# Sine tables in pairs: the second table of each pair taken from the first one's angle, and k's pad written by a transfer

## The chip, the cores and the metric

The kernel runs on one core of a Trainium2 chip. The metric is the device time of one execution in microseconds (us). Before the change the median of three runs is 212.61 us (212.39 to 212.65). Five engines work side by side, each in the order of its own program: TensorE (PE, with its weight loads PEld) multiplies matrices into PSUM, VectorE (DVE) and ScalarE (ACT) compute element by element and can read PSUM, GpSimd (POOL) makes masks and small constants and issues some transfers, SyncE (SP) issues most transfers.

## The reference

The function computes two independent branches on sequences of 2048 tokens with 576 channels and joins them along the channels.

```python
# branch A: attention in a sliding window of 8 positions, 2 apart, 32 heads of 18
qkv = x @ wqkv
idx = pos[:, None] - off[None, :]
logits = where(idx >= 0, einsum(q, k[idx]) * 18 ** -0.5, -1e9)
a = einsum(softmax(logits), v[idx]) @ wo

# branch B: a long convolution per channel
k_shift = sum(k_pad[:, t:t + S, :] * shift_k[:, 3 - t] for t in range(4))   # k_pad: three rows of zeros first
kv = k_shift * v
y = irfft(rfft(kv, 2S) * rfft(ssm_k, 2S))[:, :S] + kv * ssm_D
b = q * y
```

All inputs and the output are bf16. Three rows of zeros ahead of k are what the change calls k's pad.

## The kernel before, in words

Branch A is projections (`project_first`, lines 494 to 504, and `project`, 373 to 423), products of q and shifted k on VectorE with sums on TensorE (`logits`), a softmax, weighted sums of v (`weigh`) and the output projection (`output`). Branch B splits the sequence into four blocks of 512 tokens. For each block, `taps` (571 to 597) multiplies k's shifted rows by the tap table `skb` and then by v on VectorE; `mirror` folds the block on TensorE (L606); `x_spectrum` and `filter_spectrum` turn the blocks and the filter into the frequency domain with matmuls against tables of sines and cosines; `products` multiplies them, and `inverse` goes back with the tables `TI`, which `table_i` (449 to 460) makes from the x tables by matmuls (L455).

The order of the work is written out by hand. Each engine runs its instructions in the order in which the program emits them. From line 545 on, TensorE's units are put into a list `units` and taken from it by counts in constants such as `PLACES`; the change touches none of these. The prefix ahead of that, lines 519 to 544, is straight code: the tap table is spread by three calls of `spread_taps` (L513 matmuls, L516 evacuations by ScalarE), the x rows of the first two quarters are transposed (L467, L472; copied out by VectorE at L527 and by ScalarE at L528, L538 and L477), and four `project_first` run (L500 and L502 matmuls, an evacuation by ScalarE at L504 behind each). Sines are placed between these evacuations:

```python
    sines = [table_k(0), table_k(1)]            # 521: integer work on VectorE is emitted here
    ...
    sines += [table_x(0), table_x(1)]           # 531: and here
    ...
    project_first(0, 2)
    sines[2]()                                  # the sine itself, on ScalarE
    for n in range(2):
        project_first(1, 2 * n)
        sines[3 - 3 * n]()
```

The last table, `sines[1]`, follows the first evacuation of `project` (`with_sine`, 554 to 560). A call of `table` emits two multiply-adds (L438) and one bitwise and (L439) on VectorE, which give the phases of two vectors of 512 as integers, and returns the sine (L440) as a function: one activation of 128 x 1024, from int32 in `Ks` to bf16 in `TB`. Pools of PSUM: tag A and tag B, with two buffers each. Projections, `table_i` and the tap table's larger parts take buffers of tag A, transposes and folds those of tag B. A unit that takes a buffer waits until the buffer's former content has been evacuated.

Queues: SyncE issues x, wqkv, k and v for the front in the order of the calls in lines 196 and 244 to 259. `load_k` (198 to 215) brings k's rows for one block into `kj`, 7 rows per partition; block 0's first partition has the three rows of zeros ahead of it, which GpSimd writes with a memset (L205) before it issues the transfer of the four rows behind them (L206). The tile `xw` starts with 512 columns of zeros (L161), which serve the warming matmuls of `idle_work`; the first tap of block 0 (L577) later writes its result over them.

Of the kernel before, what the change touches and what calls it, by code (L numbers as in the profile page):

```python
# [11 lines left out]
ACT = mybir.ActivationFunctionType  # L12
ALU = mybir.AluOpType
FP32 = mybir.dt.float32
# [39 lines left out]
def view(t, offset, dims):  # L54

    return bass.AP(tensor=t.tensor, offset=t.offset + offset, ap=[list(t.ap[0])] + [list(d) for d in dims])
# [3 lines left out]
def kernel(  # L60
# [13 lines left out]
    nc = tc.nc  # L74
# [28 lines left out]
    HB = 4 * D  # L103
# [23 lines left out]
    xw = main.tile([128, 12 * HB], BF16, name="xw")  # L127
    XO = 8 * BL
    TB = main.tile([128, XO + 4 * BL], BF16, name="TB")
    TK = view(TB, 0, [[2 * BL, 2], [BL, 2], [1, BL]])  # L130
    TX = view(TB, XO, [[BL, 4], [1, BL]])
# [19 lines left out]
    def load_w(eng, comp, to=None):  # L151
        low, high = (to[:, 0:4, :], to[:, 4, :]) if to is not None else \
            (view(xw, w_at(0, comp), [[D, 4], [1, D]]), wq(4, comp, 0, D))
        eng.dma_start(low, A_wqkv[0:512, comp * D:(comp + 1) * D].rearrange("(kb p) a -> p kb a", p=128))
        for r in range(2):
            eng.dma_start(high[64 * r:64 * r + 64, :], A_wqkv[512:576, comp * D:(comp + 1) * D])

    s1 = ExitStack()
    sp1 = s1.enter_context(tc.tile_pool(name="s1", bufs=1, reuse_waits="tile"))
    zeros = view(xw, 0, [[1, 512]])  # L160
    nc.vector.memset(zeros, 0.0)  # L161
    pib = main.tile([128, 1], FP32, name="pib")
# [3 lines left out]
    nc.scalar.dma_start(skrow[96:97, :], B_shift_k.rearrange("d j -> (d j)").unsqueeze(0))  # L166
    warm = sp1.tile([128, 1], FP32, name="warm")
    nc.scalar.activation(warm[:], pib[:], ACT.Sin)
    ones96 = sp1.tile([97, 256], BF16, name="ones96")
    nc.vector.memset(ones96[:], 0.0)  # L170
    nc.vector.memset(ones96[96:97, 0:128:2], 1.0)
# [10 lines left out]
    Ks = main.tile([128, 12 * HB], BF16, name="Ks")  # L182
    xnat = view(Ks, 4 * HB, [[HB, 4], [D, 4], [1, D]])
    n_all = view(Ks, 8 * HB, [[1, 4 * HB]]).bitcast(I32).rearrange("p (n f) -> p n f", n=9)
# [8 lines left out]
    def load_x(qtr):  # L193
        nc.sync.dma_start(xnat[:, qtr], xf[512 * qtr:512 * qtr + 512, :].rearrange("(sb p) c -> p sb c", p=128))
# [3 lines left out]
    def load_k(i):  # L198

        eng = nc.sync  # L200
        kj = sp1.tile([128, 7, D], BF16, name="kj", bufs=2)
        r0 = BL * i
        low = [(0, 64)]
        if i == 0:
            nc.gpsimd.memset(kj[0:1, 0:3, :], 0.0)  # L205
            nc.gpsimd.dma_start(kj[0:1, 3:7, :], kf[0:4, :].unsqueeze(0))  # L206
            low = [(1, 49), (49, 64)]
        for a, b in ((3, 7), (0, 3)) if i == 0 else ((0, 7),):
            for p0, p1 in low:
                eng.dma_start(kj[2 * p0:2 * p1:2, a:b], bass.AP(  # L210
                    tensor=kf.tensor, offset=kf.offset + (r0 + 4 * p0 - 3 + a) * D,
                    ap=[[4 * D, p1 - p0], [D, b - a], [1, D]]))
            eng.dma_start(kj[1:128:2, a:b], bass.AP(tensor=kf.tensor, offset=kf.offset + (r0 + 256 + 3 - a) * D,
                                                    ap=[[4 * D, 64], [-D, b - a], [1, D]]))
        kjs.append(kj)
# [15 lines left out]
    rp = main.tile([128, 8], FP32, name="rp")  # L231
# [11 lines left out]

    load_w(nc.sync, 0)
    load_x(1)

    def turn_x(h):

        r0 = 1024 + 512 * h
        nc.sync.dma_start(xnat[:, 2 + h, :, 512:576], xf[r0:r0 + 512, 512:576].rearrange("(sb p) c -> p sb c", p=128))  # L250
        nc.sync.dma_start_transpose(view(xw, 6 * HB + 512 * h, [[1024, 4], [1, 512]]), xf[r0:r0 + 512, 0:512])

    load_k(0)
    load_w(nc.sync, 1)
    load_v(0)
    load_k(1)
    turn_x(0)
    turn_x(1)
# [16 lines left out]
    for h in range(2):  # L275
        f = fold[:, 64 * h:64 * h + 64]
# [156 lines left out]
    nc.vector.tensor_copy(rp[:], rp_i[:])  # L433
    nc.vector.tensor_scalar(rp[64:128, 4:8], rp[64:128, 4:8], -510.0, None, op0=ALU.add)

    def table(n_i, T, vec, cols, period, offs):
        for n in range(2):
            nc.vector.tensor_scalar(n_i[:, n, :], vec, rp[:, cols[n]:cols[n] + 1], offs[n], op0=ALU.mult, op1=ALU.add)  # L438
        nc.vector.tensor_single_scalar(n_i, n_i, period - 1, ALU.bitwise_and)  # L439
        return lambda: nc.scalar.activation(T, n_i, ACT.Sin, bias=pib[:], scale=-2.0 * np.pi / period)  # L440

    def table_k(c):
        return table(n_all[:, 2 * c:2 * c + 2, :], TK[:, c, :, :], n_all[:, 8, :], (2 + c, 2 + c), 2048, (256.0, 1792.0))

    def table_x(n):
        return table(n_all[:, 4 + 2 * n:6 + 2 * n, :], TX[:, 2 * n:2 * n + 2, :], n_all[:, 8, :], (4, 5), 4096,
              (512.0 + 1024.0 * n,) * 2)

    def table_i(s):

# [28 lines left out]
    def pair_x():  # L479
        return pp.tile([128, 2, 1024], BF16, name="ps_x", tag="B")  # L480
# [13 lines left out]
    def project_first(jp, ct0):  # L494

        ps = bank2("ps_proj", "A")
        for e in range(2):
            c0 = 128 * (ct0 + e)
            for kb in range(4):
                nc.tensor.matmul(ps[:, e, :], wq(kb, 0, c0, 128), xT(kb, 512 * jp, 512), start=(kb == 0), stop=False)  # L500
        for e in range(2):
            nc.tensor.matmul(ps[:, e, :], wq(4, 0, 128 * (ct0 + e), 128)[64 * jp:64 * jp + 64],  # L502
                             x5(0)[64 * jp:64 * jp + 64], start=False, stop=True, tile_position=(64 * jp, 0))
        nc.scalar.activation(view(q, S * ct0 + 512 * jp, [[S, 2], [1, 512]]), ps[:], ACT.Copy)  # L504

    def spread_taps(n0):
        n = min(256, D - n0)
        ps = bank2("ps_sk", "A" if n == 256 else "B")
        for h in range(0, n, 128):
            w = min(128, n - h)  # L510
            sk = skrow[:, 4 * (n0 + h):4 * (n0 + h + w)].rearrange("p (d j) -> p d j", j=4)
            for r in range(2):
                nc.tensor.matmul(ps[:, h // 128, 0:4 * w], ones96[:, 128 * r:128 * r + 128],  # L513
                                 sk if r else view(skrow, 4 * (n0 + h) + 3, [[4, w], [-1, 4]]),
                                 start=(r == 0), stop=(r == 1))
        nc.scalar.activation(skb[:, :, n0:n0 + n],  # L516
                             ps[:].rearrange("p b (d j) -> p j (b d)", j=4)[:, :, 0:n], ACT.Copy)

    spread_taps(512)
    spread_taps(0)  # L520
    sines = [table_k(0), table_k(1)]
    pts = [pair_x() for _ in range(2)]
    for n in range(2):
        transpose_x(0, pts[n], 2 * n, range(4))
# [3 lines left out]
        nc.scalar.activation(xT(2 + n, 0, 512), pts[1][:, n, 0:512], ACT.Copy)  # L528
    copy_tail(0, pts[1])
    spread_taps(256)  # L530
    sines += [table_x(0), table_x(1)]
    project_first(0, 0)
    pts = [pair_x() for _ in range(2)]
    for n in range(2):
# [125 lines left out]
    def fold_filter(m):  # L660
        kt, swapped = kTok(m), m < 2

        def unit():
            assert m in signed
            minus = minus_of(m)
            pss = [bank2("ps_rev", "A") for _ in range(2)]
            for c in range(2):
                turns = [((flip2r, flip1)[c] if swapped else flip0, 1 - c), ((identn0, identn)[c], 2 + c)]
                if not swapped:
                    turns.insert(1, ((corner2, corner)[c], c))  # L670
                for n, (w, of) in enumerate(turns):
                    for h in range(2):
                        nc.tensor.matmul(pss[c][:, h, 0:HD], w[:], kt[:, of, HD * h:HD * h + HD], start=(n == 0),  # L673
                                         stop=(n == len(turns) - 1))
            for c in range(2):
                nc.scalar.activation(halves(kt[:, c, :]), pss[c][:, :, 0:HD], ACT.Copy, scale=0.5)
                pe(0.5, "A", 0.65)
            nc.gpsimd.dma_start(view(Ks, k_at(m, 2) + 2 * D, [[1, 2 * D]]), view(Ks, k_at(m, 2), [[1, 2 * D]]),
                                accum_op=ALU.add, max_dma_last_dim=2 * D)
            nc.gpsimd.dma_start(other(m)[1:128], kt[1:128, 0, :], accum_op=ALU.add)  # L680
            nc.gpsimd.dma_start(other(m)[0:1], minus, accum_op=ALU.add)

        return (1.0, unit, f"fold{m}")
# [21 lines left out]
    def made(f, *args):  # L705
        n = len(units)
        f(*args)
        return [units.pop() for _ in range(len(units) - n)][::-1]
# [13 lines left out]
    for i in range(NBL):  # L722
# [4 lines left out]
        if i < 2:  # L727
            load_k(i + 2)
            load_v(i + 2)
# [14 lines left out]
        if i == 3:  # L744
            need("fold3")
            first = made(filter_spectrum, 3)
            now = deque(first)
            first = [[now.popleft() for _ in range(min(n, len(now)))] for n in EARLY]
            now, first = first[0] + [fold_filter(2)] + first[1] + mirrors[:1] + first[2] + mirrors[1:], list(now)
# [3 lines left out]
        for n, u in enumerate(mirrors):  # L753
            n = AT[n] if n < 2 else AT[i]
# [591 lines left out]
```

## Time and profile before

| | |
|---|---|
| median of three runs | 212.61 us |
| the profiled execution's own time | 212.5 us |
| its span, first to last instruction | 210.8 us |
| granted TensorE clock, mean | 0.998 |
| busy: TensorE, VectorE, ScalarE, GpSimd | 95%, 92%, 71%, 35% of the span |
| transfers | 39.66 MB, mean 188 GB/s |

The page of the profile and its views give times in microseconds from the span's start; L12 is line 12 of the kernel's file. In the timeline, a row has start, busy time, engine, line, operation, output and input, the number of instructions merged into it, and in brackets the idle time of the engine ahead of it with what ended it. In groups by line, the figures behind the bar are busy time and mean nanoseconds of one, then the idle time ahead of them. The chain of waits follows the work that ended last back from the end, at each step to what released it. A matmul's busy time is modelled and matmuls overlap, so a busy TensorE is not one at its peak.

### The profile page before, as it was taken

Reading aid. Unit: us, or ns where it says so; the run is one execution under the profiler, and the core shown is the slowest. Engines: PE = TensorE matmul, PEld = TensorE weight load, DVE = VectorE, ACT = ScalarE, POOL = GpSimd, SP = SyncE. Lnnn points to the kernel's source line nnn. Section 1 sums busy time; section 2 is a strip of 40 time slices with the busy share of each in tenths; the row PEclk is TensorE's granted clock in tenths of the full one; section 3 lists DMA queues with packets and bytes.
Section 4 is the critical chain, followed back from the end, with each engine's and each line's share of the span. In section 5 each row is a group of like instructions: output and inputs, shape, how many; then the busy total and the mean of one; then the engine's idle time right before and its main releaser. Section 6 shows DMA issues by size and latency. Waiting matters only on the chain.

```text
span 210.8 us, 5106 instructions
## 1 busy us (share of the span) xinstructions
PE 200.1 (95%) x2114; PEld 110.7 (53%) x2122; DVE 193.1 (92%) x146; ACT 150.5 (71%) x218; POOL 74.0 (35%) x111
## 2 busy tenths in 40 slices
PE   7999999999999999899999999999989999999891
PEld 2443443344554656564354666656555666666460
DVE  7989999999999999858889999999999849999981
ACT  3799988657684989986369788855666796775540
POOL 8999993001195516320175000002029004033000
PEclk9999999999999999999999999999999999999999
DMA  6999998999639336999999997587559995985133
GB/s 201 303 328 231 266 342 280 170 192 182 151 75 122 48 40 87 180 181 171 235 225 238 194 234 159 105 208 185 153 223 255 239 322 110 214 243 182 28 113 111
DMA packets 35396, 39.66 MB, mean 188 GB/s; under 512 B 17619, under 2 KB 29007, under 8 KB 35374
## 3 DMA queue, kind: packets, MB, share of 16 engines
q1 hardware_dynamic: 26812, 24.88, 47.2%
q0 software_dynamic: 6096, 11.96, 30.4%
q10 hardware_dynamic: 2466, 2.51, 3.5%
q8 instruction: 16, 0.26, 0.5%
q14 instruction: 6, 0.05, 0.1%
HBM read 13.11 MB, written 4.72 MB: 85 GB/s over the span
## 4 chain that ended last, share of the span: by engine, by line
PE 80%; ACT 10%; DVE 5%; issue 2%; DVEq 0%; ACTq 0%
PE ps_proj L378 16%; PE ps_z L1126 9%; PE ps_wo L1029 8%; PE ps_acc L973 7%; PE ps_inv L1158 7%; PE ps_fx L776 6%; PE ps_log L847 4%; PE ps_proj L500 3%; PE ps_fk L627 3%; PE ps_proj L382 3%; PE ps_proj L389 3%; ACT Ks L695 3%; PE ps_rev L673 2%; PE ps_fk L628 1%; ACT qk L977 1%
## 5 line engine op out<-in xcount | busy, mean ns | idle before, releaser
L378 PE MATMUL ps_proj<-xw 128*128 128x512 bf16 x153 | 37.4, 380 | 0.6 <-issue 0.3
L832 DVE TENSOR_TENSOR av<-qk 128x4096 bf16<-128x4096 bf16 (+1 forms) x16 | 31.7, 2013 | 2.8 <-PE ps_log L847 2.8
L378 PEld LDWEIGHTS <-xw 128*128 128x128 bf16 x160 | 14.0, 97 | 20.5 <-issue 6.2
L1099 DVE TENSOR_TENSOR qk<-xw,Ks 128x2304 bf16<-128x2304 bf16 x14 | 18.5, 1355 | 2.5 <-PE ps_inv L1158 2.4
L1139 ACT ACTIVATE av<-ps_z 128x768 bf16<-128x768 f32 x20 | 15.3, 808 | 6.2 <-PE ps_z L1126 6.2
L414 ACT ACTIVATE qk<-ps_proj 128x1024 bf16<-128x1024 f32 x14 | 14.3, 1023 | 7.6 <-PE ps_proj L389 3.3
L695 ACT ACTIVATE Ks<-ps_fk 128x576 bf16<-128x576 f32 x32 | 18.6, 717 | 1.3 <-PE ps_fk L628 1.3
L577 DVE TENSOR_TENSOR tB<-kj,skb 128x4608 bf16<-128x4608 bf16 (+1 forms) x8 | 19.3, 2417 | 0.1
L778 ACT ACTIVATE xw<-ps_fx 128x576 bf16<-128x576 f32 x32 | 18.4, 666 | 0.0
L776 PE MATMUL ps_fx<-xw,TB 128*128 128x288 bf16 x128 | 18.0, 286 | 0.2
L1055 POOL DMA_DIRECT2D Ks<-Ks x3 | 3.7, 1218 | 41.1 <-PE ps_wo L1029 28.7
L1029 PE MATMUL ps_wo<-qk 128*128 128x288 bf16 x128 | 17.8, 287 | 0.0
L627 PE MATMUL ps_fk<-Ks,TB 128*128 128x384 bf16 x62 | 16.9, 326 | 0.8 <-ACT Ks L695 0.7
L414 ACT ACTIVATE v<-ps_proj 128x1024 bf16<-128x1024 f32 x9 | 9.3, 1029 | 9.3 <-PE ps_proj L378 4.3
L973 PE MATMUL ps_acc<-av,ident 64*64 64x512 bf16 x160 | 15.3, 377 | 0.0
L628 PE MATMUL ps_fk<-Ks,TB 128*128 128x192 bf16 x62 | 15.2, 245 | 0.0
L776 PEld LDWEIGHTS <-TB 128*128 128x128 bf16 x128 | 12.0, 97 | 6.0 <-issue 2.9
L1029 PEld LDWEIGHTS <-qk 128*128 128x128 bf16 x128 | 11.6, 98 | 5.6 <-issue 3.0
L1158 PE MATMUL ps_inv<-av,TI 128*128 128x288 bf16 (+1 forms) x96 | 13.6, 293 | 0.6 <-ACT av L1139 0.6
L1161 ACT ACTIVATE v<-ps_inv 128x576 bf16<-128x576 f32 (+1 forms) x14 | 9.5, 677 | 6.3 <-PE ps_inv L1158 6.3
L977 ACT ACTIVATE qk<-ps_acc 128x1024 bf16<-128x1024 f32 x8 | 8.2, 1024 | 8.0 <-PE ps_acc L973 8.0
L956 DVE TENSOR_TENSOR av<-Ks,v 128x4096 bf16<-128x4096 bf16 x6 | 13.6, 2286 | 0.2 <-PE ps_acc L973 0.2
(199 smaller groups left out, 471.3 us busy)
## 6 DMA issues: line engine op xcount, KB each, us to landing
Ks<-Ks POOLq DMA_DIRECT2D x9, 576.0 KB, 7.1
TB<-av SPq DMA_DIRECT2D x12, 256.0 KB, 5.5
kj<-in_B_k_dram SPq DMA_DIRECT2D x6, 504.0 KB, 6.1
vt<-in_B_v_dram SPq DMA_DIRECT2D x8, 288.0 KB, 5.2
Ks<-av SPq DMA_DIRECT2D x8, 256.0 KB, 5.5
Ks<-Ks SPq DMA_DIRECT2D x3, 576.0 KB, 6.1
Ks<-in_A_x_dram SPq DMA_DIRECT2D x2, 576.0 KB, 5.2
xw<-in_A_wqkv_dram SPq DMA_DIRECT2D x2, 576.0 KB, 5.9
```

The costliest lines, as they stand in the source:

```text
L378: nc.tensor.matmul(ps[:, jp, :], wq(kb, comp, 128 * ct, 128), xT(kb, 1024 * jj + 512 * jp, 512), **se)
L414: nc.scalar.activation(view(t, o + pad + 1024 * jj, [[512, 2], [1, 512]]), ps[:], ACT.Copy)
L577: dve(2304 * n, lambda: nc.vector.tensor_tensor(to, view(kj, row * D, [[D, n], [D, 4], [1, D]]), view(skb, row * D, [[D, n], [0, 4], [1, D ...
L627: nc.tensor.matmul(o[:, 0:2], w, rhs[:, 0:2], start=start, stop=stop)
L695: nc.scalar.activation(view(Ks, k_at(m, cs ^ (m & 1)) + 96 * gi, [[768, 3], [384, 2], [1, 96]]), acc3(ps), ACT.Copy, scale=(PSG, MSG)[cs][ ...
L776: nc.tensor.matmul(ps[:, pm, 0:HD], TX[:, 2 * pm + c, 128 * gi:128 * gi + 128], kv[:, 2 * c + pm, HD * h:HD * h + HD], start=(c == 0), sto ...
L832: return P, at, step, dve(1024 * nj, lambda: nc.vector.tensor_tensor(view(P, at, [[step, 4], [256, nj], [1, 256]]), view(t, o + 256 * hh, ...
L973: nc.tensor.matmul(acc[64 * o:64 * o + 64, h, :], ident[64 * h:64 * h + 64, 64 * h:64 * h + 64], view(P, 256 * u, [[2048, 2], [1, 256]])[6 ...
L1029: nc.tensor.matmul(ps[:, r, 0:HD], oT(hh, 2 * c + r, t)[:, o:o + 128], wo[:, t // 2, t % 2, HD * h:HD * h + HD], start=(t == 0 and h == 0) ...
L1099: r = dve(3 * QTR, lambda: nc.vector.tensor_tensor(pr, view(xw, HB * XG[i] + QTR * t, [[HB, 3], [1, QTR]]), view(Ks, k_at(j - i, 0) + QTR ...
L1126: nc.tensor.matmul(view(acc[r], 512 * h, [[192, 2], [96, 2], [1, 96]])[o:o + 64], w[64 * h:64 * h + 64, 64 * h:64 * h + 64], pr[64 * h:64 ...
L1158: nc.tensor.matmul(ps[:, c, 0:n], TI[:, sl, pm, 128 * c:128 * c + 128], Y(j, pm)[:, sl, c0:c0 + n], start=(pm == 0 and sl == 0), stop=(sl ...
```

## The change

The second table of each pair is no longer computed from integer phases of its own. `table` now makes the phases of a pair's first table only. On ScalarE `first` takes the sine of the angle and, in a second activation, the absolute value of the same angle, which it writes as fp32 into the place where the second table's phases stood. `second` takes the sine of plus or minus this absolute value plus a bias of minus or plus a quarter turn, which gives minus the cosine for x and the cosine for k. The biases are two new columns, `quarter_turn`, set by GpSimd ahead of its other work. A pair is now formed over the two column sets, so a first or a second table covers both; the places at which `sines` are called are the same, and `sines[2]` and `sines[0]` are now the two `first` functions.

The three rows of zeros ahead of k's block 0 are now copied from the zeros at the start of `xw` by a transfer that ScalarE's queue issues. The call `load_k(0)` stands a few lines higher, ahead of the definition of `turn_x`, between the same other calls.

```diff
     nc.scalar.activation(warm[:], pib[:], ACT.Sin)
+    quarter_turn = {}
+    for sign in (-1, 1):
+        quarter_turn[sign] = sp1.tile([128, 1], FP32, name="quarter_turn", bufs=2)
+        nc.gpsimd.memset(quarter_turn[sign][:], float(np.float32(-0.5 * sign * np.pi)))
...
-            nc.gpsimd.memset(kj[0:1, 0:3, :], 0.0)
+            nc.scalar.dma_start(kj[0:1, 0:3, :], view(xw[0:1], 0, [[0, 4], [1, 432]]))
             nc.gpsimd.dma_start(kj[0:1, 3:7, :], kf[0:4, :].unsqueeze(0))
...
     load_x(1)
+    load_k(0)
 
     def turn_x(h):
...
-    load_k(0)
     load_w(nc.sync, 1)
...
-    def table(n_i, T, vec, cols, period, offs):
+    def table(at, cols, period, off, T, sign):
+        n_i = n_all[:, at:at + 2, :]
         for n in range(2):
-            nc.vector.tensor_scalar(n_i[:, n, :], vec, rp[:, cols[n]:cols[n] + 1], offs[n], op0=ALU.mult, op1=ALU.add)
+            nc.vector.tensor_scalar(n_i[:, n, :], n_all[:, 8, :], rp[:, cols + n:cols + n + 1], off, op0=ALU.mult,
+                                    op1=ALU.add)
         nc.vector.tensor_single_scalar(n_i, n_i, period - 1, ALU.bitwise_and)
-        return lambda: nc.scalar.activation(T, n_i, ACT.Sin, bias=pib[:], scale=-2.0 * np.pi / period)
...
+        mag = view(Ks, 8 * HB, [[1, 4 * HB]]).bitcast(FP32).rearrange("p (n f) -> p n f", n=9)[:, at + 2:at + 4, :]
+
+        def first():
+            nc.scalar.activation(T[0], n_i, ACT.Sin, bias=pib[:], scale=-2.0 * np.pi / period)
+            nc.scalar.activation(mag, n_i, ACT.Abs, bias=pib[:], scale=-2.0 * np.pi / period)
+
+        def second():
+            nc.scalar.activation(T[1], mag, ACT.Sin, bias=quarter_turn[sign][:], scale=float(sign))
+
+        return [first, second]
+
+    def table_k():
+        return table(0, 2, 2048, 256.0, [TK[:, :, n, :] for n in range(2)], -1)
+
+    def table_x():
+        return table(4, 4, 4096, 512.0, [TX[:, 2 * n:2 * n + 2, :] for n in range(2)], 1)
...
-    sines = [table_k(0), table_k(1)]
+    sines = table_k()
...
-    sines += [table_x(0), table_x(1)]
+    sines += table_x()
```

More of the change, by code (lines that the diff above doesn't have):

```diff
@@ L434 @@
     nc.vector.tensor_scalar(rp[64:128, 4:8], rp[64:128, 4:8], -510.0, None, op0=ALU.add)
-    def table(n_i, T, vec, cols, period, offs):
+    def table(at, cols, period, off, T, sign):
+        n_i = n_all[:, at:at + 2, :]
         for n in range(2):
-            nc.vector.tensor_scalar(n_i[:, n, :], vec, rp[:, cols[n]:cols[n] + 1], offs[n], op0=ALU.mult, op1=ALU.add)
+            nc.vector.tensor_scalar(n_i[:, n, :], n_all[:, 8, :], rp[:, cols + n:cols + n + 1], off, op0=ALU.mult,
+                                    op1=ALU.add)
         nc.vector.tensor_single_scalar(n_i, n_i, period - 1, ALU.bitwise_and)
[L440 to L447, printed above, removed]
+        mag = view(Ks, 8 * HB, [[1, 4 * HB]]).bitcast(FP32).rearrange("p (n f) -> p n f", n=9)[:, at + 2:at + 4, :]
[9 more added lines that the diff above has]
+        return table(4, 4, 4096, 512.0, [TX[:, 2 * n:2 * n + 2, :] for n in range(2)], 1)
     def table_i(s):
```

## The prediction

> **What bounds the kernel now.** The page comes first: how full each engine is, and which engine the chain that ended last runs on.
>
> ```profile
> span 210.8 us, 5106 instructions
> PE 200.1 (95%) x2114; PEld 110.7 (53%) x2122; DVE 193.1 (92%) x146; ACT 150.5 (71%) x218; POOL 74.0 (35%) x111
> PE 80%; ACT 10%; DVE 5%; issue 2%; DVEq 0%; ACTq 0%
> ```
>
> TensorE carries 80% of the chain, and VectorE is nearly as full (92%) with only 5% of it. ScalarE's 71% is an average, so the question is what ScalarE does where the sine tables are made. The second view is the chain in order of time (start, length, what), for the two places that the change touches.
>
> ```profile
> 5.75 0.86 DVE Ks L438 x2
> 6.63 0.69 DVE Ks L439
> 7.33 0.34 DVE xw L527
> 7.80 1.91 PE ps_proj L500 x8
> ...
> 20.89 1.02 ACT qk L414
> 21.91 1.04 ACT TB L440
> 22.95 1.01 ACT qk L414
> ...
> 24.00 0.38 PE ps_proj L378
> ```
>
> The first place is the front: VectorE's integer work for the k tables (L438, L439) stands ahead of the copy L527 that the first projection waits for. The second is 20.89 to 24.00: the chain leaves TensorE and runs through ScalarE, where a sine (L440) stands between two evacuations (L414) and TensorE's next projection starts just behind the second. The third view is ScalarE's timeline around it (start, busy, then the idle time before it and its releaser).
>
> ```profile
> 11.63 1.94 ACT L538 ACTIVATE xw<-ps_x 128x1024 bf16<-128x1024 bf16 x2 [0.32 <-PE ps_x L472]
> 13.59 0.59 ACT L477 ACTIVATE xw<-ps_x 64x512 bf16<-64x512 bf16 x1
> 14.21 1.02 ACT L504 ACTIVATE qk<-ps_proj 128x1024 bf16<-128x1024 f32 x1
> 15.13 1.14 ACT L440 ACTIVATE TB<-Ks,pib 128x1024 bf16<-128x1024 int32 x1
> 16.36 1.02 ACT L504 ACTIVATE qk<-ps_proj 128x1024 bf16<-128x1024 f32 x1
> 17.28 1.14 ACT L440 ACTIVATE TB<-Ks,pib 128x1024 bf16<-128x1024 int32 x1
> 18.73 1.02 ACT L504 ACTIVATE qk<-ps_proj 128x1024 bf16<-128x1024 f32 x1 [0.30 <-PE ps_proj L502]
> ...
> 21.81 1.14 ACT L440 ACTIVATE TB<-Ks,pib 128x1024 bf16<-128x1024 int32 x1
> 22.93 1.02 ACT L414 ACTIVATE qk<-ps_proj 128x1024 bf16<-128x1024 f32 x1
> ...
> 26.26 1.02 ACT L414 ACTIVATE qk<-ps_proj 128x1024 bf16<-128x1024 f32 x1 [0.24 <-PE ps_proj L389]
> ```
>
> From 14.21 to 23.95 (22.93 + 1.02) ScalarE runs one lane in program order: five evacuations with a sine behind each of the first four. An evacuation to the next start is 0.92 (15.13 - 14.21, again 17.28 - 16.36), the last one counts its full 1.02, and a sine takes 1.04 of the lane in the chain of waits. That is 4 x 0.92 + 1.02 + 4 x 1.04 = 8.86 us of work in 9.74 us, so the lane has 0.88 us of slack, and its end releases TensorE.
>
> **The change, part by part.** *Integer work on VectorE.* The groups of the first 13 us price it (busy, mean ns):
>
> ```profile
> L438 DVE TENSOR_SCALAR Ks<-Ks,rp 128x512 int32<-128x512 int32 x8 | 3.6, 494 | 0.0
> L439 DVE TENSOR_SCALAR Ks<-Ks 128x1024 int32<-128x1024 int32 x4 | 2.8, 709 | 0.1
> ```
>
> Four of the eight L438 and two of the four L439 go: half of 3.6 + 2.8, so 3.2 us. Half of that, one table's 0.86 + 0.69 = 1.55 us on the chain, stood ahead of L527. What is late next is TensorE and the transfers:
>
> ```profile
> 6.42 1.04 PE L513 MATMUL ps_sk<-tB,ones 97*128 97x512 bf16 x4
> 7.80 1.91 PE L500 MATMUL ps_proj<-xw 128*128 128x512 bf16 x8 [0.35 <-DVE xw L527]
> ```
>
> TensorE is busy until 7.46 (6.42 + 1.04) with L513 in any case, so L500 comes 0.34 us earlier at most, and not at all if its weights are only just there. I take the 0.34, since 0.35 is what the wait itself shows, and keep 0 as the other end. It reaches ScalarE, because L538 at 11.63 waits for TensorE's transposes.
>
> The second half of the saving, the x tables' integer work, stood ahead of the taps:
>
> ```profile
> 10.41 0.75 DVE L439 TENSOR_SCALAR Ks<-Ks 128x1024 int32<-128x1024 int32 x1
> 11.88 1.36 DVE L577 TENSOR_TENSOR xw<-kj,skb 128x2304 bf16<-128x2304 bf16 x1 [0.72 <-DMA kj<-in_B_k_dram]
> ...
> 21.32 1.36 DVE L597 TENSOR_TENSOR xw<-xw,vt 128x2304 bf16<-128x2304 bf16 x1
> ```
>
> VectorE already waits 0.72 us there for k's transfer, so this half is worth nothing on that line: the wait grows from 0.7 to some 3.9 us and the first tap stays at 11.88. From there VectorE runs without a pause as before, and block 0's products end at 22.68.
>
> *The extra pass on ScalarE.* Per pair of tables there were two sines; now there are sine, absolute value, sine. So there are two more 128x1024 passes, one behind the x sine at about 15.1 and one behind the first k sine at about 19.7. No absolute value runs in this trace. The nearest rows are the sines: same size, same 4-byte source in SBUF, same bias by pointer; each takes 1.14 us. Between start and next start a sine takes 1.04 (chain) to 1.12 (22.93 - 21.81, though that L414 also had to wait for its matmuls). A gain is excluded, as the pass is added and nothing else on ScalarE goes. I take 1.04, since the row with 1.12 contains some waiting, and keep 1.12 for the range. The Trainium skill (ScalarE: Activation LUTs, What ACT_TABLE_LOAD costs) gives such a pass 280 ns + 0.833 ns per column whatever the function, less 93 ns when back to back; the estimate from it is 1133 - 93 = 1040 ns, and the sum by it is the one below; with 1.12 it would be 0.48 more.
>
> Sum for the lane: the evacuations take 4 x 0.92 + 1.02 = 4.70, six passes at 1.04 take 6.24, together 10.94. From 14.21 less 0.34 that ends at 24.81 instead of 23.95: **+0.86 us**. For this the lane must be packed, that is, no evacuation may wait for its matmuls. Starts would be 13.87, 16.87 (+0.92 + 2 x 1.04), 18.83, 21.83 and 23.79, against matmuls of before that were done by 16.3, 18.7, 20.9 and 22.9 (each at most the start of the evacuation shown): it is packed. With six passes at 1.12 it is 4.70 + 6.72 = 11.42 and the end 25.29, +1.34; without the 0.34 at the front the two are +1.20 and +1.68.
>
> What then waits: L414 at the lane's end frees one of the two buffers of tag A, and the projection at 24.00 needs it. Meanwhile TensorE has this to do:
>
> ```profile
> 22.82 0.68 PE L606 MATMUL ps_fold<-xw,fold 128*64 128x288 bf16 x8
> 23.34 0.61 PE L455 MATMUL ps_ti<-ident,TB 128*64 128x128 bf16 x16
> ```
>
> Both keep their place (the fold follows block 0's products at 22.68; L455 needs the buffer that the earlier L414 frees, at 21.83 + 1.02 = 22.85), so they end by 23.95 as before, and TensorE stands idle from there to some 24.86. Behind the stall ScalarE has 0.24 us of idle time at 26.26 as before, so the lane is level again and the shift stays as it is. Can it be made up later?
>
> ```profile
> 24.00:54.00 30.00, 29.84 (x207) 12.69 (x210) 29.48 (x18) 22.09 (x31) 11.12 (x22) 1.00 1.04 238
> PE ps_fk L627 <- ACT Ks L695: 0.7, 1, 0.7
> PE ps_z L1126 <- ACT qk L977: 0.8, 1, 0.8
> ```
>
> The first line is the stretch behind it (length, then busy us of TensorE, weight loads, VectorE, ScalarE and GpSimd): TensorE is busy 29.84 of 30 us. The next two are TensorE's longest waits behind it, from the table of waits, and both are for evacuations of its own results, which shift with it. So I let the whole 0.86 us through.
>
> *k's pad.* A memset on GpSimd becomes a transfer on ScalarE's queue.
>
> ```profile
> 2.37 1.53 POOL L205 MEMSET kj<- 1x1728 bf16 x1
> 3.85 0.87 POOL L206 DMA_DIRECT2D kj<-in_B_k_dram  x1
> ...
> 0.83 0.53 ACTq L166 DMA_DIRECT2D tB<-in_B_shift_k_dram  x1
> ...
> 3.62 0.38 ACT L516 ACTIVATE skb<-ps_sk 128x256 bf16<-128x256 f32 x1 [0.73 <-PE ps_sk L513]
> ...
> kj<-in_B_k_dram POOLq DMA_DIRECT2D x1, 4.5 KB, 6.2
> ```
>
> GpSimd's queue moves up by 1.53 less two memsets of a column each (0.1 at most), its transfer L206 too; it lands at 3.85 + 6.2 = 10.05 now, ahead of the 11.88 at which the taps start, so that is worth nothing. The new transfer is issued behind the warming sine at 2.89, costs its 0.53 as L166's did, and fits the 0.73 that L516 waits: nothing on ScalarE. It reads the zeros in xw, which the first tap at 11.88 overwrites, so that tap must wait for it as well. Landing as the small GpSimd transfer did, at about 2.9 + 6.2 = 9.1, it leaves 2.8 us; it would cost something only from a landing beyond 9 us. The call that loads block 0 of k moves across a function definition, which issues nothing, so SyncE's queue stays in its order.
>
> The profiled execution took 212.5 us, beside the median of 212.61: 212.5 + 0.86 = 213.4 for that run, **213.5 us** against the median.
>
> **The rivals.**
>
> *The delay is made up, or is smaller.* If a wait later in the kernel is for something that does not shift (a transfer, VectorE), TensorE's delay shrinks there. For it: VectorE is busy 29.48 of those 30 us, so it runs as a second line close behind. Against it: no wait of any length names it. The lowest end here has the lane costing nothing and the 0.34 kept, 212.3; the highest has half the delay left, 213.0.
>
> *Faster: the first tap starts earlier.* If k's rows landed sooner, VectorE could start when the last part of the tap table is there, at about 9.0 (L516 behind its matmuls, which end at 7.46, and two copies), up to 2.9 us earlier, and if VectorE paces the kernel, the end moves with it. For it: VectorE's fill from 12 us on. Against it: the transfers that fill kj are issued by SyncE in the same order, and TensorE carries the chain. It decides if the first tap starts more than about 0.5 us ahead of 11.88 and VectorE, not TensorE, sets the pace; with a third of the 2.9, 211.6.
>
> *The absolute value is not in the table that the sine uses.* Then each of the two absolute values needs another table and the sine behind it the first one again: four loads.
>
> ```profile
> L168 ACT ACT_TABLE_LOAD x1 | 1.3, 1283 | 1.4 <-PEq L1330 1.4
> ```
>
> At 1.28 us each, all in the packed lane: 213.5 + 5.1 = 218.6. Against it: copies run between the sines without a load. The Trainium skill (ScalarE: Activation LUTs, Table sets) says that absolute value is in every set, so by it this cannot happen; no run shown here has the function.
>
> **How the numbers follow.** About 0.2%, 0.43 us, is what a measurement of this kernel can tell from no change. The packed lane gets 0.70, with its own range 213.05 (half of the 0.86 lost later) to 214.3 (+1.68). A delay made up gets 0.15, and lies within 0.2%; the early tap 0.12, faster; the table loads 0.03, slower. So faster 0.12, same 0.15, slower 0.73. The range goes from 212.2, which takes in the second case, to 214.5, a little over the highest lane; left out are the early tap, the table loads and some of the first case's edge, under 2 in 10.
>
> **What would show it.** Right: two activations of absolute value of about 1.14 us in ScalarE's timeline, L500's first start at about 7.46, the taps still at 11.9 with a longer wait for kj, the evacuations from 16.87 on without idle time before them, and a gap on TensorE of 0.9 us ahead of the projection that was at 24.00. Wrong: the taps moving up; L538 not moving up by 0.3; ScalarE waiting for matmuls inside the lane; or the gap at 24 us present while the end stays put, which would mean that a later wait had taken it up.

## The result, and the profile after

The changed kernel takes 212.94 us in the median of 20 executions, beside 212.38 us for the kernel before, taken with it. The ratio is 1.0031, with a 95% interval of 1.0017 to 1.0045: it is slower by 0.3%, or 0.7 us (0.4 to 1.0 us by the interval). The forecast was 213.5 us and 0.86 us slower.

The profiled execution took 212.86 us with a span of 211.1 us. First ScalarE's timeline, the columns being start, busy time, engine, line and operation, and in brackets the idle time ahead (the line numbers are those of the changed file: L518 is what was L504, L418 was L414, L449 is the first sine, L450 the absolute value, L453 the second sine):

```profile
13.89 1.02 ACT L518 ACTIVATE qk<-ps_proj 128x1024 bf16<-128x1024 f32 x1
14.81 1.14 ACT L449 ACTIVATE TB<-Ks,pib 128x1024 bf16<-128x1024 int32 x1
15.85 1.14 ACT L450 ACTIVATE Ks<-Ks,pib 128x1024 f32<-128x1024 int32 x1
16.89 1.01 ACT L518 ACTIVATE qk<-ps_proj 128x1024 bf16<-128x1024 f32 x1
17.80 1.14 ACT L453 ACTIVATE TB<-Ks,quarter_turn 128x1024 bf16<-128x1024 f32 x1
18.83 1.01 ACT L518 ACTIVATE qk<-ps_proj 128x1024 bf16<-128x1024 f32 x1
19.74 1.15 ACT L449 ACTIVATE TB<-Ks,pib 128x1024 bf16<-128x1024 int32 x1
20.78 1.14 ACT L450 ACTIVATE Ks<-Ks,pib 128x1024 f32<-128x1024 int32 x1
21.82 1.01 ACT L418 ACTIVATE qk<-ps_proj 128x1024 bf16<-128x1024 f32 x1
22.72 1.15 ACT L453 ACTIVATE TB<-Ks,quarter_turn 128x1024 bf16<-128x1024 f32 x1
23.76 1.02 ACT L418 ACTIVATE qk<-ps_proj 128x1024 bf16<-128x1024 f32 x1
...
27.09 1.02 ACT L418 ACTIVATE qk<-ps_proj 128x1024 bf16<-128x1024 f32 x1 [0.25 <-PE ps_proj L393]
```

No evacuation in the lane waits for its matmuls any more. The lane ends at 24.78 us (23.76 + 1.02) where it ended at 23.95, and the idle 0.25 us behind it is the same as before. TensorE's timeline at the same place:

```profile
20.68 1.90 PE L382 MATMUL ps_proj<-xw 128*128 128x512 bf16 x8
23.25 0.68 PE L620 MATMUL ps_fold<-xw,fold 128*64 128x288 bf16 x8 [0.68 <-DVE xw L611]
23.74 0.64 PE L469 MATMUL ps_ti<-ident,TB 128*64 128x128 bf16 x16
24.83 1.89 PE L382 MATMUL ps_proj<-xw 128*128 128x512 bf16 x7 [0.45 <-ACT qk L418]
```

The projection that started at 24.00 starts at 24.83. Between it and the end, the chain of waits has the same pieces, all 0.82 us later: the matmuls of the spectral sums that came at 189.24 come at 190.06. The last pieces of the two chains, before and then after:

```profile
189.24 2.75 PE ps_z L1126 x64
192.13 1.12 issue
193.25 0.91 DVE qk L1099
...
206.75 0.47 DVEq L1341
```

```profile
190.06 2.72 PE ps_z L1140 x64
192.79 1.09 PE ps_inv L1172 x8
...
207.17 0.46 DVEq L1355
```

In the profiled execution of the kernel before, VectorE held up the last stage: the chain leaves TensorE at 192.13, and its last piece starts 17.51 us behind the one at 189.24. After, it stays on TensorE there and the last piece starts 17.11 us behind. That is why the two spans differ by 0.3 us only while TensorE is 0.82 us late. Not every execution has these 0.4 us: two runs below, one of them the kernel before with only the pad changed, reach the same piece at 189.25 and 189.35 and then end like the changed kernel. Of the 20 executions of the kernel before, 8 took 212.08 to 212.18 us and the others 212.32 or more; which of these VectorE held up is not known.

At the front, VectorE's timeline shows the saving and where it went:

```profile
4.20 0.69 DVE L445 TENSOR_SCALAR Ks<-Ks 128x1024 int32<-128x1024 int32 x1
5.80 0.76 DVE L541 COPY xw<-ps_x 128x512 bf16<-128x512 bf16 x2 [0.91 <-PE ps_x L481]
6.48 0.96 DVE L443 TENSOR_SCALAR Ks<-Ks,rp 128x512 int32<-128x512 int32 x2
7.47 0.75 DVE L445 TENSOR_SCALAR Ks<-Ks 128x1024 int32<-128x1024 int32 x1
12.32 1.36 DVE L591 TENSOR_TENSOR xw<-kj,skb 128x2304 bf16<-128x2304 bf16 x1 [4.10 <-DMA kj<-in_B_k_dram]
```

The copies come 1.4 us sooner. The first tap does not (12.32 for 11.88): VectorE sits 4.1 us idle until k's rows have landed.

### The profile page after: what moved, and what is told of

The parts are those of the page before. It is cut to its first block, busy times and chain, and to the rows that moved or that the text cites. A ratio compares the mean times of both kernels' runs of the same rounds, so it can differ in the third digit from the quotient of the medians.

```text
span 211.1 us, 5105 instructions
## 1 busy us (share of the span) xinstructions
PE 199.7 (95%) x2114; PEld 110.8 (52%) x2122; DVE 189.4 (90%) x140; ACT 152.1 (72%) x220; POOL 58.4 (28%) x112
## 4 chain that ended last, share of the span: by engine, by line
PE 75%; ACT 9%; DVE 5%; DMA 5%; issue 2%; SPq 1%; DVEq 0%; ACTq 0%
PE ps_proj L382 15%; PE ps_z L1140 10%; PE ps_wo L1043 8%; PE ps_inv L1172 7%; PE ps_acc L987 7%; PE ps_fx L790 6%; PE ps_log L861 4%; PE ps_fk L641 3%; DMA xw<-in_A_wqkv_dram 3%; ACT Ks L709 3%; PE ps_proj L386 3%; PE ps_proj L393 2%; DMA kj<-in_B_k_dram 2%; DVE xw L595 2%; DVE tB L591 2%
## 5 line engine op out<-in xcount | busy, mean ns | idle before, releaser
L418 ACT ACTIVATE qk<-ps_proj 128x1024 bf16<-128x1024 f32 x14 | 14.3, 1022 | 7.5 <-PE ps_proj L393 3.2
L418 ACT ACTIVATE v<-ps_proj 128x1024 bf16<-128x1024 f32 x9 | 9.3, 1029 | 9.3 <-PE ps_proj L382 4.3
```

Of the source, the lines that this page charges most:

```text
L418: nc.scalar.activation(view(t, o + pad + 1024 * jj, [[512, 2], [1, 512]]), ps[:], ACT.Copy)
```

## The experiments

All ratios are to the kernel before, with 95% intervals; the changed kernel's is 1.0031 (1.0017 to 1.0045).

**The two halves of the change, one at a time.** The transfer for the pad alone:

```diff
-            nc.gpsimd.memset(kj[0:1, 0:3, :], 0.0)
+            nc.scalar.dma_start(kj[0:1, 0:3, :], view(xw[0:1], 0, [[0, 4], [1, 432]]))
```

> The kernel before with k's pad written by ScalarE's transfer and nothing else changed. Theory (the extra pass in ScalarE's lane is the whole cost): no second pass, so the lane ends at 23.95 us or 0.3 earlier; the time stays within 0.2% of before. Rival (the transfer costs by itself): in the changed kernel SyncE waited 0.8 us ahead of block 0's second set of k loads and the first tap came at 12.32 instead of 11.88. If the transfer is the reason, the first tap is late by 0.4 us here too, block 0's fold, which had no slack before (it ran at 22.82 behind products that ended at 22.68), moves to about 23.25, the projection from 24.00 to about 24.4, and the time is up to 0.4 us (0.2%) longer.

The ratio is 1.0013 (0.9990 to 1.0036), medians 212.35 and 212.38 us. The projection starts at 24.12, the first tap at 11.89, and the end of its chain is one of the two spoken of above:

```profile
189.35 2.72 PE ps_z L1126 x64
192.07 1.09 PE ps_inv L1158 x8
...
206.45 0.47 DVEq L1341
```

No cost of the transfer can be seen, within 0.1% by the medians. The interval, which is one of means, takes in up to 0.36%, since one of the eleven executions took 215.16 us and the others 212.05 to 212.78; that one was not profiled. SyncE waited 0.6 us ahead of k's second set of loads here too, yet the first tap was on time, so this wait is not what made the tap late in the changed kernel.

The tables alone:

```diff
-            nc.scalar.dma_start(kj[0:1, 0:3, :], view(xw[0:1], 0, [[0, 4], [1, 432]]))
+            nc.gpsimd.memset(kj[0:1, 0:3, :], 0.0)
```

> The changed kernel with k's pad by GpSimd's memset as before, so that only the tables differ from before. Theory: the lane is as packed as in the changed kernel, the projection that was at 24.00 us starts at 24.8 to 24.9, and the time is that of the changed kernel, 0.3% above before. Rival (the transfer has a part in the cost): the time lies clearly below the changed kernel's, at +0.1% or less. The first tap should be back at 11.9 us.

The ratio is 1.0032 (1.0021 to 1.0043), that of the changed kernel: the tables are the whole cost. The lane starts at 13.72 here and ends at 24.61, and TensorE's projection follows it:

```profile
24.67 1.89 PE L382 MATMUL ps_proj<-xw 128*128 128x512 bf16 x7 [0.47 <-ACT qk L418]
```

The first tap came at 12.12, late again without the transfer. Over the profiles of this study it lies between 11.74 and 12.32 whatever the pad; where in it these 0.6 us come from was not followed up.

**The same passes at another place.** The two absolute values leave `first` and are emitted where their phases are ready:

```diff
+        def magnitude():
+            nc.scalar.activation(mag, n_i, ACT.Abs, bias=pib[:], scale=-2.0 * np.pi / period)
...
-            nc.scalar.activation(mag, n_i, ACT.Abs, bias=pib[:], scale=-2.0 * np.pi / period)
...
-        return [first, second]
+        return [first, second, magnitude]
...
     sines = table_k()
+    sines.pop()()
...
     sines += table_x()
+    sines.pop()()
```

> The changed kernel with its two absolute values emitted as soon as their phases are made, which is where ScalarE waited: k's behind the second evacuation of the tap table (at about 5.9 us), x's behind the third (at about 9.0). The number of passes is the same. Theory: the lane from 13.9 us on has four sines again and 0.88 us of slack, so the projection is released by block 0's fold and no longer by ScalarE: fold at about 23.25 (the first tap stays at 12.3), projection at 24.4 instead of 24.83; the time is some 0.4 us (0.2%) below the changed kernel. Rival (the number of passes on ScalarE counts, not their place): the time stays that of the changed kernel.

The ratio is 1.0008 (0.9987 to 1.0029), the median 212.30 us: by the median the cost is gone with the same work on ScalarE. The interval is again wide by one execution, of 214.82 us, and does not exclude a part of it. In its profile, the two passes (L449) stand in front of the lane, and the lane has idle time again:

```profile
5.90 1.14 ACT L449 ACTIVATE Ks<-Ks,pib 128x1024 f32<-128x1024 int32 x1
...
9.27 1.15 ACT L449 ACTIVATE Ks<-Ks,pib 128x1024 f32<-128x1024 int32 x1
...
18.32 1.02 ACT L520 ACTIVATE qk<-ps_proj 128x1024 bf16<-128x1024 f32 x1 [0.31 <-PE ps_proj L518]
```

TensorE now waits for the other thing that this place needs, block 0's products:

```profile
22.95 0.68 PE L624 MATMUL ps_fold<-xw,fold 128*64 128x288 bf16 x8 [0.47 <-DVE xw L615]
23.44 0.64 PE L471 MATMUL ps_ti<-ident,TB 128*64 128x128 bf16 x16
24.01 1.90 PE L382 MATMUL ps_proj<-xw 128*128 128x512 bf16 x7
```

The projection is back at 24.01. It came 0.4 us sooner than I had expected for this run because the first tap was at 11.99 and not at 12.3.

With the memset for the pad as well:

> As the run with the early absolute values, and k's pad by GpSimd's memset again. Theory: lane with slack and first tap at 11.9 us, so the fold comes at about 22.8 and the projection at 24.0, as before: the time is that of before within 0.2%, 0.3% below the changed kernel. Rival (the place of the passes does not count): the time stays that of the changed kernel.

The ratio is 0.9996 (0.9987 to 1.0004), the projection at 24.01, the piece of the spectral sums at 189.25 and the end of the chain at 206.35. This is the time of the kernel before, and its interval is clear of the 1.0021 to 1.0043 of the tables alone, from which this run differs only in the place of the two passes.

**One pass in the lane.** Only k's absolute value is taken out:

```diff
+        if sign == -1:
+            nc.scalar.activation(mag, n_i, ACT.Abs, bias=pib[:], scale=-2.0 * np.pi / period)
         def first():
...
-            nc.scalar.activation(mag, n_i, ACT.Abs, bias=pib[:], scale=-2.0 * np.pi / period)
+            if sign == 1:
+                nc.scalar.activation(mag, n_i, ACT.Abs, bias=pib[:], scale=-2.0 * np.pi / period)
```

> The changed kernel with only k's absolute value moved out of the lane, to about 5.9 us; x's stays behind x's first sine. Theory (slack of 0.88 us and 0.34 us of head start, against passes of 1.04): five passes and the evacuations end at 13.87 + 4.70 + 5.20 = 23.77 us, ahead of the 24.0 at which TensorE gets to its projection anyway, so one pass in the lane costs nothing and the time is that of before within 0.2%. Rival (each pass in the lane has its price, in proportion): half of the changed kernel's 0.3% is left, the projection at about 24.4 us and no idle time before the evacuations.

The ratio is 1.0000 (0.9990 to 1.0011), so the first pass is free and the second carries the price: the cost is what exceeds the slack, not a price per pass. The profiled execution shows something else beside it:

```profile
5.09 1.91 PE L485 MATMUL ps_x<-ident,Ks 128*128 128x128 bf16 x16
...
24.67 1.89 PE L382 MATMUL ps_proj<-xw 128*128 128x512 bf16 x7 [0.17 <-ACT qk L418]
```

The first 16 transposes, which took 1.06 us in the profile of before and 1.07 in that of the changed kernel, took 1.91 us, and the lane starts 0.9 us later than in the changed kernel (14.75 for 13.89). The lane's length from 14.75 to 24.62 is 9.87 us, beside the 9.90 of the expectation (4.70 + 5.20). So the head start of the front is not there in every execution, and in this one the single pass held TensorE up by 0.17 us; the next section comes back to it.

**More passes in the lane.** Each absolute value twice, and then x's alone twice:

```diff
             nc.scalar.activation(mag, n_i, ACT.Abs, bias=pib[:], scale=-2.0 * np.pi / period)
+            nc.scalar.activation(mag, n_i, ACT.Abs, bias=pib[:], scale=-2.0 * np.pi / period)
```

> The changed kernel with each absolute value computed twice over, so that the lane has eight passes instead of six. Theory: a pass takes 1.04 us of the packed lane, so the projection moves from 24.83 by 2.08 to 26.9 us, and all of it reaches the end: 2.0 to 2.1 us (1.0%) above the changed kernel, 1.3% above before. Rival (a later wait takes up part of TensorE's delay, as the smaller step in the changed kernel's time than in its projection, 0.6 against 0.83 us, could suggest): 1.5 us or less above the changed kernel.

In the profiled execution the projection and the end came where the theory put them. TensorE's projection, and then the end of the chain:

```profile
26.90 1.89 PE L382 MATMUL ps_proj<-xw 128*128 128x512 bf16 x7 [1.31 <-ACT qk L418]
```

```profile
192.13 2.72 PE ps_z L1141 x64
...
209.23 0.46 DVEq L1356
```

The projection is 2.07 us later than in the changed kernel, the spectral sums 2.07 and the end 2.06: all of a delay of TensorE at 25 us reaches the end. That the delay is 2.07 is luck, though. The lane started 0.29 us sooner here than in the changed kernel and was 2.36 us longer (13.60 to 26.85 us, beside 13.89 to 24.78), so a repeated pass cost 1.18 us and not 1.04. The second of two passes that write the same place starts 1.17 us behind the first:

```profile
15.56 1.14 ACT L450 ACTIVATE Ks<-Ks,pib 128x1024 f32<-128x1024 int32 x1
16.73 1.15 ACT L451 ACTIVATE Ks<-Ks,pib 128x1024 f32<-128x1024 int32 x1
17.79 1.00 ACT L519 ACTIVATE qk<-ps_proj 128x1024 bf16<-128x1024 f32 x1
```

And while that execution took 214.92 us, five others took 216.9 to 217.6, the ratio being 1.0217 (1.0182 to 1.0252). The five have a mean granted TensorE clock of 0.991, the profiled one 0.999. Two more runs looked into that.

> The changed kernel with x's absolute value computed twice, k's once: seven passes in the lane. With eight, the profiled execution took the 2.07 us that two passes cost, 214.9 us, but five of six took 216.9 to 217.6 at a mean granted TensorE clock of 0.991 instead of 0.999. Theory A (each pass costs its 1.04 us, and the rest is a drop of the granted clock that sets in only when TensorE stands idle for long enough): projection at about 25.9 us; 1.0 us above the changed kernel, 213.7 to 214, in executions at a clock of 0.995 or more, and 2 to 2.6 us more than that in any execution at 0.991. Theory B (the extra is a cost of the passes themselves, by a wait that the profiled execution happened to miss): about half of the extra in all executions, 215 us, with the clock as in the changed kernel.

With seven passes, all five executions took 214.1 to 214.9 us at clocks of 0.994 to 0.997, the ratio 1.0102 (1.0085 to 1.0119), which is 1.4 us above the changed kernel's median of 212.94 where 1.0 was expected. The projection stands at 26.05, 1.22 us later than in the changed kernel, behind a lane that began at 13.92: the repeated pass accounts for 1.2 of the 1.4. None fell on 0.991. Of seven and eight passes, only executions with eight have the extra 2 us and the low clock, but all five of those ran on one chip, and the seven passes on another.

> The kernel with eight passes once more, for a profile of an execution at the lower clock. Theory A: if it falls on 0.991, the granted clock is below full in one stretch of a few microseconds behind the gaps at 19 to 27 us (gaps of 0.8, 1.2 and 1.3 us in the first profile), the matmuls there take up to twice as long, and the time is about 217 us. Theory B: the clock is full behind the gaps, and a wait further on explains the extra 2 us.

This one, on the chip of the seven passes, came out at 215.2 us with a granted clock of 1.000, so it has nothing to show of the drop. With its lane starting at 13.88 the projection came at 27.19 and the last piece of the chain at 209.52, 2.36 and 2.35 us later than in the changed kernel: twice the 1.18, and again all of it at the end. TensorE's gaps were the same as in the first profile:

```profile
PE ps_proj L382 <- ACT qk L418: 1.3, 1, 1.3
PE ps_ti L470 <- ACT qk L418: 1.2, 1, 1.2
PE ps_proj L382 <- ACT qk L519: 0.8, 1, 0.8
```

Theory A is supported by the clocks that go with the times, and by nothing else, and this is weak. In all twelve traces half clock is recorded only behind TensorE's last matmul, in the last 0 to 2.8 us of the span, and that alone makes their means of 0.993 to 1.000. A mean of 0.991 would be some 3.9 us at half clock (an estimate, 2 x 0.009 x 215 us). Whether these lie inside the work, and cost the time, or at its end, and only follow from it, was not seen.

**Can both kernels be beaten?** In the run with early absolute values and the transfer TensorE reached the fold 0.5 us before its data; with the memset, whose profiled front was slower, it did not. So the transposition of the x tables was put ahead of the fold, with the memset for the pad:

```diff
-            n = AT[n] if n < 2 else AT[i]
+            n = 3 if (i, n) == (0, 0) else AT[n] if n < 2 else AT[i]
```

> Both absolute values early, the memset for the pad, and the transposition of the x tables (its matmuls) placed ahead of block 0's first fold in TensorE's order instead of behind it. With the lane free, TensorE reaches this place 0.4 us sooner than before in one of the two runs with early absolute values and then waits 0.5 us for VectorE's products. Theory: the table's matmuls fill that wait and the projection starts at 23.6 to 23.7 us where TensorE is early; but VectorE's first tap is at 11.9 us still, and its products for the logits at 66 us, which were ready 0.1 us before TensorE asked for them, hold TensorE back then: 0 to 0.1 us gained at the end, the time that of before within 0.2%. Rival (TensorE alone paces the kernel): 0.4 us below before.

The ratio is 0.9999 (0.9987 to 1.0011). The projection did come at 23.62, 0.4 us ahead of the kernel before, and in the profiled execution it was lost again at 68 us. There it was not VectorE's products, as I had expected, but the filter's transfers, in the chain of this profile (its execution, 213.19 us, is the longest of the twelve):

```profile
41.62 1.85 PE ps_proj L382 x8
43.47 0.90 SPq L231
44.41 4.20 SPq L231
48.65 8.26 DMA Ks<-in_B_ssm_k_dram
...
64.68 4.03 DMA Ks<-Ks
68.75 1.15 PE ps_rev L691 x8
```

The chain leaves TensorE at 43.5 us and comes back at 68.75 through the filter's loads (L231) and the moves of its first rows. In the profile of before the same matmuls (there L673) start at 68.38, so this execution was by then 0.4 us behind. The other eleven have a median of 212.11 us, that of the kernel before being 212.13; where they lost the 0.4 us is not shown.

Last, the two small loads of the projection weights went to ScalarE's queue in addition, to let SyncE come to k sooner:

```diff
-            eng.dma_start(high[64 * r:64 * r + 64, :], A_wqkv[512:576, comp * D:(comp + 1) * D])
+            (eng if comp else nc.scalar).dma_start(high[64 * r:64 * r + 64, :], A_wqkv[512:576, comp * D:(comp + 1) * D])
```

> As the run with the fold behind the table's matmuls, and the two small loads of the projection's last weight rows issued by ScalarE's queue instead of SyncE's, so that SyncE comes to block 0's k loads 1.2 us sooner (their issue takes 2 x 0.6 us). Theory (VectorE's first tap waits for these loads, and with the lane free VectorE and TensorE pace the kernel together): the first tap comes 0.3 to 1.2 us sooner, and TensorE's 0.4 us are kept: 0.2 to 0.4 us (0.1 to 0.2%) below before. Rival (the loads land no sooner, since the transfer engines are full in this stretch): first tap at 11.9 us and the time that of before.

The ratio is 1.0007 (0.9993 to 1.0021) and the first tap came at 11.81. SyncE issued its first load of k at 2.40 us instead of 3.77, and the tap came no sooner than the 11.80 of the run without this move: issuing k's loads sooner did not land them sooner, as the rival said. Whether TensorE keeps its 0.4 us this profile cannot tell, since its transposes took 1.89 us and the projection came at 24.35. No version here is measurably faster than the kernel before.

## Why the prediction was right

*What bounds.* Right. The cost is ScalarE's lane from 14 to 24 us, in which the sines and evacuations alternate. Taking the absolute values out of it removes the cost (0.9996); taking the pad's transfer out does not (1.0032).

*The price of a pass and the packed lane.* Right to a few hundredths. The starts were forecast as 13.87, 16.87, 18.83, 21.83 and 23.79 and came at 13.89, 16.89, 18.83, 21.82 and 23.76; a pass takes 1.04 us from start to start (15.85 to 16.89). The estimate from the Trainium skill (ScalarE: Activation LUTs, What ACT_TABLE_LOAD costs), 1.04 us, agrees with it. The Trainium skill (ScalarE: Activation LUTs, Table sets) has absolute value in every set. This trace agrees: the absolute value at 15.85 follows the sine at 14.81 without a load.

*The whole shift reaches the end.* Right for this place: 24.83 against 24.00 at the projection and 0.82 us at 190 us. Against the run with early absolute values and the memset, whose projection is at 24.01, it is 0.82 us at the last piece too (207.17 and 206.35). With more passes, 2.07 and 2.36 us at the projection came through whole.

*The head start of 0.34 us.* Right for the profiled execution, where the first projection started at 7.36 us and the lane 0.32 us sooner, but wrong as a fixed number, so that it came out is in part luck. It rests on the transposes at 5.1 us taking 1.06 us, and in four of the ten profiled executions of experiments they took 1.60 to 1.91. The traces show why. The 16 transposes start 0.11 us apart until the trace's record of the granted clock begins, at full clock, and 0.06 us apart from there. It begins at 5.07 us in the profile of before and at 4.22 in the one after, but at 6.21, 6.44, 7.00 and 7.50 in those four, in the order of their 1.60, 1.71, 1.89 and 1.91. In the kernel before, VectorE's integer work kept the first projection back to 7.80 in any case, so it covered transposes of nearly 1.6 us (with 1.60 and 1.71 us TensorE came to it at 7.83 and 7.94). With the tables changed this cover is gone, and the first projection lies between 7.21 and 8.37. The interval of 0.4 to 1.0 us takes in both the 0.86 us forecast and the 0.7 us measured, so their difference is not explained further.

*k's pad and the first tap.* The cost of nothing was right as far as the runs can tell: with the tables changed, the ratio is 1.0031 with the transfer and 1.0032 without. The transfer was issued at 1.46 us, ahead of the warming sine and not behind it at 2.89, and took 0.72 us in place of 0.53. What taking the memset away does to VectorE was not foreseen (last section). That the first tap stays at 11.88 was wrong in the profile after: it came at 12.32, and TensorE's gap was therefore two gaps, 0.68 us ahead of the fold and 0.45 us ahead of the projection, in place of one of 0.9. It cost nothing, as the lane ended later still.

*The rivals.* A delay made up later does not show on TensorE's path; the smaller difference of the two spans, which looks like it, is the 0.4 us that VectorE cost in the profiled execution of before. How many executions of before have these, and so how much of the 0.82 us they take out of the measured difference, stays open. The early tap was excluded by the transfers, as argued. No table was loaded.

## What to carry to other kernels

Price an added instruction by the slack of the lane in which it stands, not by the engine's share of the span: ScalarE was busy 71% of the span and the added 2.1 us were 1% of the span, yet 0.9 us of the lane's 9.74 was free and the rest came through to the end. One pass fitted and the second did not; the same two passes 7 and 15 us earlier, where the engine waited, were free. Work saved on an engine that then waits for a transfer is worth nothing, and an edit that removes such cover can show what it hid.

## What was not expected of the hardware

GpSimd and VectorE hold each other up. GpSimd's memset of 1 x 1728 elements, 1.53 us in the kernel before, ran beside VectorE's cast of 128 x 8 at 2.85 us, which took 1.07 us and ended at 3.92, just behind the memset (3.90); in the changed kernel, without it, the cast took 0.10:

```profile
2.85 0.10 DVE L437 CAST rp<-rp_i 128x8 f32<-128x8 int32 x1
```

With the memset back it took 1.13 in all four runs that had it, and in the runs without it 0.10 to 0.22. The other way, GpSimd's masks of 64 x 32 (L294), 1.32 us each at 14.65 and 18.64 beside VectorE's taps, took 0.20 and 0.21 in the changed kernel, where they fell into VectorE's wait from 8.2 to 12.3 us; GpSimd's busy time went from 74.0 to 58.4 us. The masks are in the chain of neither profile. The cast was on the path in the profile of before, ahead of VectorE's integer work:

```profile
2.93 1.00 DVE rp L433
```

The run with the transfer alone saves most of it, and its copies come 0.7 us sooner (6.55 for 7.24), but TensorE came to its first projection only at 7.94 there, so nothing was gained. The Trainium skill (SBUF — State Buffer, SBUF: two separate sides) has the two engines share a pair of ports which, in some of VectorE's modes, one instruction holds to its end; the 1.07 us beside 0.10 agree with that.

With three gaps of 0.8 to 1.3 us on TensorE between 18 and 27 us, five of seven executions were 1.7 to 2.7 us longer than the other two, at a mean granted clock of 0.991 against 0.999 and 1.000. With two gaps of 0.8 and 1.3 us none of five were, but on another chip. The Trainium skill (TensorE: Matmul & The Clock Gate, Part 1) has the clock halved behind an idle window of about 3.4 us. No single gap in the two profiles is that long (1.31 us at most), and neither caught a drop, so no run here shows whether that is the mechanism.
